# One repeated load taken out, and the startup and the first turn of a fused attention and gated feed-forward kernel put in another order

## The chip, the cores and the metric

The kernel runs on one core of a Trainium2 chip. The metric is the device time of one execution, in microseconds (us). The kernel before takes 296.58 us (median of four runs, 295.89 to 297.06). Times of a stage are read from one profiled execution of each kernel, whose clock starts with the span; a span is about 2 us shorter than the device time.

A core has engines that run side by side: TensorE multiplies matrices, VectorE and ScalarE work on elements, and GpSimd issues most of the loads here. A DMA is a transfer between memories. The granted clock is the share of TensorE's full speed that the profile shows, 1.00 or 0.50 here. A warming product is a matrix product whose result is not used.

Runs of one and the same kernel differ here by up to 2%. Over four jobs the kernel before gave 292.4 to 298.1 us. A good part of what follows is about the reason, so single microseconds are compared only between kernels that ran in one job, or stage by stage in the profiles. All runs compared are "fast", which here means within 1.5% of the fastest run of the same kernel.

## The reference

```python
# attention: window of 16 around each position, plus 24 block summaries (max of k, mean of v)
scores_l = scale * q @ k.T;  masked where |i-j| >= 16
scores_s = scale * q @ k_sum.T + log(32)
a = softmax(concat(scores_l, scores_s));  attn = a @ concat(v, v_sum)
# gated feed-forward on x = attn, 3072 tokens x 512
out = x + sigmoid(x @ w_res) * ((gelu(x @ w_gate) * (x @ w_val)) @ w_out)
```

There are 4 batches, 8 heads, 768 positions of 64 dimensions, and 1536 inner features.

## The kernel before

The work is cut into 8 units, each half a batch (384 tokens). A unit is: scores and exponentials for four head pairs, attention products, transposes of the normed result `xn` into `xT`, twelve blocks of gate and value products (`g`, `vv`), then residual products (`r`) and output products (`f`). While one unit's `r` and `f` run, the next unit's attention is woven in; I call this the turn. In these traces TensorE takes its matmuls in the order of the program (in the changed kernel a transpose whose input is ready at 20.25 starts at 22.16, behind a product that waits), so an order of statements is an order of waits.

Unit 0 has nothing to be woven into. Its attention is the startup. This is its second half, as it was before:

```python
        firsts = [(w, fo, None) for fo in range(2) for w in (w_gate, w_val)]
        for hp in range(NP):                       # four head pairs
            av_part(0, hp, st, blocks=True)        # TensorE: attention products with the block summaries
            av_norm(hp, st)                        # VectorE: reciprocal and multiplication -> xn
            if hp:
                xt_step(0, hp - 1, st, *(AO if hp % 2 else TT), nc.scalar.copy)   # TensorE transposes, ScalarE copies
            if hp > 1:
                firsts = [(w, fo, half_fo(st, w, fo, hp - 2, hp - 1, acc)) for w, fo, acc in firsts]
        firsts = [(w, fo, half_fo(st, w, fo, NP - 2, NP - 1, acc)) for w, fo, acc in firsts]
        xt_step(0, NP - 1, st, *TT, nc.scalar.copy)
        # ... constants ...
        load_batch(1)
        load_batch(1)
```

The transpose of pair `hp - 1` stands behind the block products of pair `hp`, and the gate and value products of pair `hp - 2` stand behind that transpose. So while ScalarE copies one transposed pair, TensorE has another pair's work.

`load_batch(1)` stands twice. Each call takes the next buffers of its pool, and the program reads what the second call loaded. In the startup's first half two of the four pairs' scores are masked by VectorE after the exponential, and two by adding a large negative mask in the accumulator with a TensorE product (`ident` times `nmask`).

The softmax here doesn't subtract the row's maximum and nothing guards it: scores larger than these inputs give would overflow.

## Time and profile before

| stage (from the timeline) | from | to | us |
|---|---|---|---|
| startup: first transpose of k to `g` of the third inner block | 6.99 | 28.66 | 21.67 |
| unit 0's other inner blocks, to the first scores of the turn | 28.66 | 42.87 | 14.21 |
| unit 0's turn, to unit 1's first `g` | 42.87 | 59.83 | 16.96 |
| unit 1, to unit 2's first `g` | 59.83 | 102.29 | 42.46 |

The windows view of the kernel before for these four stages. Columns: the stretch, its length, busy time of each engine with its number of instructions, then the granted TensorE clock, the share of the DMA engines and GB/s.

```profile
6.99:28.66 21.67, 17.03 (x280) 9.87 (x280) 12.65 (x50) 12.33 (x21) 15.68 (x22) 0.76 1.80 182
28.66:42.87 14.21, 14.21 (x112) 8.43 (x112) 8.92 (x18) 6.16 (x14) 6.64 (x8) 1.00 1.32 203
42.87:59.83 16.96, 14.07 (x158) 7.31 (x158) 9.38 (x21) 8.39 (x11) 6.97 (x9) 1.00 1.97 179
59.83:102.29 42.46, 38.34 (x386) 20.51 (x388) 23.91 (x59) 20.43 (x30) 13.87 (x18) 0.92 1.61 166
```

Of these four stages, the clock is under 1.00 in the startup and in unit 1. On the page of the kernel before, the rows of busy tenths of TensorE and of its clock say where, in 40 slices of 7.4 us:

```profile
PE   8589996949999999999999999999999999999993
...
PEclk9867999987999999999999999999999999999998
```

From the tenth slice to the last but one TensorE is busy for 90% or more of each.

The chain of waits of the kernel before, in unit 1 (start, length, what):

```profile
54.68 10.43 DMA k_sb<-in_k_dram
...
65.15 0.85 PE tp L174 x16
66.00 1.39 PE g L295 x4
```

TensorE had nothing left to do at about 61.3 and stood until the second copy of batch 1's k had landed at 65.15. The four gate products after the transposes take 1.39 us, about twice the 0.65 of a dense unit: the clock is at half. In the GpSimd timeline of the kernel before both loads can be seen, the first one long before it is needed and never read, the second behind the seven value loads of the first call:

```profile
31.17 0.79 POOL L87 DMA_DIRECT2D k_sb<-in_k_dram  x1 [0.46 <-DMA w_val<-in_moe_w_val_dram]
...
54.68 0.79 POOL L87 DMA_DIRECT2D k_sb<-in_k_dram  x1 [4.05 <-PE xp L282]
```

The chain of waits of the kernel before in the second half of the startup:

```profile
21.29 0.57 DVE xn L273
...
21.90 0.34 PE xp L282 x3
22.25 0.32 PE ao L263 x12
...
22.98 0.32 PE g L295
...
27.03 0.18 PE xp L282 x3
...
27.23 0.49 ACT xT L284
...
28.66 0.48 PE g L295 x2
```

Between 21.90 and 27.03 nearly every piece is TensorE's own work. Only the last copy (0.49) is waited for. The windows view for the two clock windows around it shows what the clock did:

```profile
19.35:22.77 3.42, 2.47 (x47) 1.41 (x46) 1.89 (x6) 1.44 (x4) 2.69 (x4) 1.00 1.46 199
22.77:26.18 3.41, 3.41 (x26) 1.76 (x24) 1.49 (x6) 0.96 (x2) 1.91 (x3) 0.50 1.45 194
```

### The profile page before, as it was taken

How to read it: one execution, taken by the hardware profiler on the slowest of the kernel's cores; microseconds unless marked ns; L12 is line 12 of the kernel's file. 1: busy time of each engine (PE TensorE's matmuls, PEld its weight loads, DVE VectorE, ACT ScalarE, POOL GpSimd, SP SyncE). 2: the span in 40 equal slices, each digit the busy share in tenths (PEclk: the TensorE clock that was granted, in tenths of full speed). 3: DMA queues.
4: the chain of work that ended last, by engine and by line, in shares of the span. 5: the costliest groups of instructions: out<-in, count | busy, mean ns of one | idle time of the engine just before them, and what ended most of it. 6: DMA issues, size and time to landing. Idle time of an engine off the chain costs nothing.

```text
span 294.4 us, 6276 instructions
## 1 busy us (share of the span) xinstructions
PE 275.7 (94%) x2602; PEld 149.8 (51%) x2624; DVE 174.6 (59%) x431; ACT 138.4 (47%) x214; POOL 52.3 (18%) x74
## 2 busy tenths in 40 slices
PE   8589996949999999999999999999999999999993
PEld 3444553525555555555554555555554565456541
DVE  3745734635556787387655786386655784575333
ACT  2853459004646443564656433654655434643410
POOL 7965632543620300013000000000000000000000
PEclk9867999987999999999999999999999999999998
DMA  6999999999999380009000110001000110010001
GB/s 91 168 184 196 201 206 205 148 234 165 195 137 191 88 85 0 2 36 129 2 0 3 71 38 1 2 36 73 2 0 3 71 38 0 2 71 38 0 36 71
DMA packets 51867, 23.72 MB, mean 81 GB/s; under 512 B 32128, under 2 KB 48768, under 8 KB 51840
## 3 DMA queue, kind: packets, MB, share of 16 engines
q0 software_dynamic: 48384, 17.04, 58.4%
q1 hardware_dynamic: 3456, 6.29, 5.7%
q8 instruction: 20, 0.33, 0.5%
q14 instruction: 7, 0.06, 0.1%
HBM read 34.08 MB, written 6.29 MB: 137 GB/s over the span
## 4 chain that ended last, share of the span: by engine, by line
PE 89%; DMA 4%; ACT 3%; DVE 2%; issue 1%; DVEq 0%; ACTq 0%
PE g L295 23%; PE vv L295 21%; PE f L323 19%; PE r L313 7%; PE tp L174 4%; PE ao L263 4%; DMA k_sb<-in_k_dram 4%; PE s L239 3%; PE vs L204 3%; PE xp L282 2%; PE wp L337 2%; ACT P L243 1%; PE s L232 1%; ACT kW L181 1%; ACT L243 0%
## 5 line engine op out<-in xcount | busy, mean ns | idle before, releaser
L295 PE MATMUL g<-xT,w_gate 128*128 128x384 bf16 x384 | 82.6, 332 | 0.7 <-ACT xT L284 0.6
L301 ACT ACTIVATE ge<-g 128x384 f32<-128x384 f32 x96 | 47.0, 491 | 73.5 <-DVE gvT L302 38.8
L302 DVE TENSOR_TENSOR gvT<-ge,vv 128x384 bf16<-128x384 f32 x96 | 53.0, 553 | 46.3 <-PE vv L295 44.4
L295 PE MATMUL vv<-xT,w_val 128*128 128x384 bf16 x384 | 80.5, 330 | 0.0
L323 PE MATMUL f<-w_out,gvT 128*128 128x512 bf16 x274 | 65.7, 379 | 1.4 <-issue 1.0
L295 PEld LDWEIGHTS <-w_val 128*128 128x128 bf16 x384 | 38.0, 99 | 26.9 <-issue 2.9
L295 PEld LDWEIGHTS <-w_gate 128*128 128x128 bf16 x384 | 35.4, 99 | 24.6 <-issue 3.5
L323 PEld LDWEIGHTS <-gvT 128*128 128x128 bf16 x288 | 27.1, 98 | 30.4
L243 ACT ACTIVATE P<-s,bias_t 128x768 bf16<-128x768 f32 x32 | 28.9, 902 | 28.7 <-PE s L239 28.6
L96 POOL DMA_DIRECT2D vext<-in_v_dram x35 | 28.8, 827 | 60.7 <-PE ao L263 41.9
L247 DVE TENSOR_TENSOR P<-P,maskt 128x768 bf16<-128x768 bf16 x30 | 16.7, 556 | 18.4 <-ACT P L243 18.4
L313 PE MATMUL r<-w_res,xT 128*128 128x512 bf16 x88 | 24.4, 381 | 0.4
L328 DVE SCALAR_TENSOR_TENSOR th<-th,f 128x512 f32<-128x512 f32 x24 | 16.3, 681 | 8.9 <-PE f L323 8.9
L181 ACT COPY kW<-tp 128x768 bf16<-128x768 bf16 x16 | 12.8, 801 | 18.0 <-PE tp L174 18.0
L273 DVE TENSOR_TENSOR xn<-ao,rz 128x384 bf16<-128x384 f32 x32 | 17.8, 558 | 1.1
L316 ACT ACTIVATE th<-r 128x512 f32<-128x512 f32 x24 | 14.3, 595 | 8.8 <-PE r L313 8.4
L195 ACT COPY qT<-tp 128x768 bf16<-128x768 bf16 (+1 forms) x20 | 13.3, 676 | 8.4 <-PE tp L174 8.4
L263 PEld LDWEIGHTS <-P 128*64 128x64 bf16 (+2 forms) x432 | 10.2, 116 | 13.6 <-DVE P L247 5.1
L330 DVE SCALAR_TENSOR_TENSOR o<-th,xn 128x512 f32<-128x512 f32 x24 | 16.6, 692 | 0.8
L239 PE MATMUL s<-qT,kW 64*128 64x64 bf16 x384 | 11.5, 194 | 3.7 <-DVE kW L191 1.9
L271 DVE RECIPROCAL rz<-ao 128x6 f32<-128x6 f32 x32 | 6.2, 192 | 14.7 <-PE ao L263 14.6
L185 DVE TENSOR_TENSOR km<-kW 128x384 bf16<-128x384 bf16 x16 | 5.7, 353 | 13.5 <-ACT kW L181 13.3
(62 smaller groups left out, 200.9 us busy)
## 6 DMA issues: line engine op xcount, KB each, us to landing
out_dram<-o SPq DMA_DIRECT2D x24, 256.0 KB, 2.1
vext<-in_v_dram POOLq DMA_DIRECT2D x25, 128.0 KB, 12.5
k_sb<-in_k_dram POOLq DMA_DIRECT2D x4, 768.0 KB, 10.0
q_sb<-in_q_dram POOLq DMA_DIRECT2D x4, 768.0 KB, 13.9
w_gate<-in_moe_w_gate_dram POOLq DMA_DIRECT2D x6, 256.0 KB, 8.7
w_val<-in_moe_w_val_dram POOLq DMA_DIRECT2D x6, 256.0 KB, 8.9
w_out<-in_moe_w_out_dram POOLq DMA_DIRECT2D x3, 512.0 KB, 14.1
k_sb<-in_k_dram POOLq DMA_DIRECT2D x2, 384.0 KB, 5.9
```

What stands on the lines that cost most here:

```text
L96: nc.gpsimd.dma_start(out=dst, in_=v[b, :, lo:hi, :].rearrange("h p d -> p h d"))
L239: nc.tensor.matmul(s[:, hh, t * QT:(t + 1) * QT], kw[ps, tt, :], qt[ps, tt * QT:(tt + 1) * QT], start=not first, stop=True, skip_group_che ...
L243: nc.scalar.activation(P.rearrange("p a t q -> p a (t q)"), s[:, :, 0:TU], AF.Exp, scale=scale, bias=bias_t[:])
L247: nc.vector.tensor_mul(Pf, Pf, maskt.unsqueeze(1).to_broadcast([128, 2 * HT, QT]))
L263: nc.tensor.matmul(ao[64 * e:64 * e + 64, sub, hh, :], P[rows, hh, t, :], rhs, start=blocks is None or (not blocks and sub == 0 and hh == ...
L273: nc.vector.tensor_mul(xn, ao[:, :, :, 0:D], rz.to_broadcast([128, NSUB, 2, D]))
L295: nc.tensor.matmul(acc[:, 0:TU], w[:, ko, fs], st["xT"][:, ko, :], start=(ko == 0), stop=(ko == KO - 1))
L301: nc.scalar.activation(ge[:], g[:, 0:TU], AF.Gelu)
L302: nc.vector.tensor_mul(gvT[:, fo, :], ge[:], vv[:, 0:TU])
L313: nc.tensor.matmul(r[:], st["xT"][:, ko, ss], w_res[:, ko, :], start=(ko == 0), stop=(ko == KO - 1))
L323: nc.tensor.matmul(st["f", sub][:], gvT[:, fo, ss], w_out[:, fo, :], start=(fo == 0), stop=(fo == FO - 1))
L330: nc.vector.scalar_tensor_tensor(o[:], th[:], 0.5, st["xn"][:, sub, :], ALU.mult, ALU.add)
```

## The change

It has four parts.

- **Load**: the second `load_batch(1)` goes.
- **Front**: all four first scores are masked by TensorE; 13 warming products at the start and 3 more in the gap ahead of the first scores, in place of 16 at the start; the block means of the values are spread differently.
- **Loop**: block products and norms of all four pairs first, then transpose, copy and products pair by pair.
- **Turn**: in unit 0's turn two residual products come ahead of the second scores, and output products are cut in twos.

```diff
-        keep_warm(16)
+        keep_warm(13)
 ...
-        for hp in range(NP):
+        for hp in range(2):
             k_step(0, hp, *MM)
             q_step(qa, 0, 0, TU, hp, *MM)
-            if hp:
-                s_step(0, hp - 1, st, hp > 2)
-            ...
+        s = mask_step()
+        keep_warm(3)
+        s_step(0, 0, st, s)
+        ...                              # the like for pairs 1 to 3: k and q of the next pair, mask, scores
+        vs = vsum_sum(0, *MM, range(0, 2))
 ...
         for hp in range(NP):
             av_part(0, hp, st, blocks=True)
             av_norm(hp, st)
-            if hp:
-                xt_step(0, hp - 1, st, *(AO if hp % 2 else TT), nc.scalar.copy)
-            if hp > 1:
-                firsts = [(w, fo, half_fo(st, w, fo, hp - 2, hp - 1, acc)) for w, fo, acc in firsts]
-        firsts = [(w, fo, half_fo(st, w, fo, NP - 2, NP - 1, acc)) for w, fo, acc in firsts]
-        xt_step(0, NP - 1, st, *TT, nc.scalar.copy)
+        for hp in range(NP):
+            xt_step(0, hp, st, *(TT if hp % 2 else AO), nc.scalar.copy)
+            if hp < NP - 1:
+                firsts = [(w, fo, half_fo(st, w, fo, hp, hp + 1, acc)) for w, fo, acc in firsts]
 ...
         load_batch(1)
-        load_batch(1)
 ...
                 s_step(n, 0, nst)
                 res_step(st, 0)
+                res_step(st, 1)
                 s_step(n, 1, nst)
-                res_step(st, 1)
+                res_step(st, 2)
                 s_step(n, 2, nst)
+                ffn_step(st, gvT, 0, 0, 2)
                 av_step(n, 0, nst)
-                res_step(st, 2)
+                ffn_step(st, gvT, 0, 2, 4)
 ...
```

More of the change, by code (lines that the diff above doesn't have):

```diff
@@ L224, in vsum_bc, with mask_step, s_step @@
             nc.vector.tensor_copy(vext[b % 2][96:128, lo:hi, 2 * hp:2 * hp + 2, 0:D], src)
-        def s_step(u, hp, st, first=False):
+        def mask_step():
+            s = ps_s.tile([128, 2, 512], F32, tag="s", name="s")
+            for hh in range(2):
+                nc.tensor.matmul(s[:, hh, 0:TU].rearrange("p (t q) -> p t q", t=HT), ident[:],
+                                 nmask.unsqueeze(1).to_broadcast([128, HT, QT]),
+                                 start=True, stop=False, skip_group_check=True)
+            return s
+        def s_step(u, hp, st, s=None):
             b, half = u // 2, u % 2
-            s = ps_s.tile([128, 2, 512], F32, tag="s", name="s")
+            first = s is not None
+            if not first:
+                s = ps_s.tile([128, 2, 512], F32, tag="s", name="s")
             kw, qt = kW[b % 2][hp], qT[b % 2][hp]
-            if first:
-                for hh in range(2):
-                    nc.tensor.matmul(s[:, hh, 0:TU].rearrange("p (t q) -> p t q", t=HT), ident[:],
-                                     nmask.unsqueeze(1).to_broadcast([128, HT, QT]),
-                                     start=True, stop=False, skip_group_check=True)
             for t in range(HT):
@@ L363 @@
         st = new_unit()
-        keep_warm(16)
+        keep_warm(13)
         nc.scalar.activation(pre[:], bias_t[0:1, :], AF.Exp)
-        for hp in range(NP):
+        for hp in range(2):
             k_step(0, hp, *MM)
             q_step(qa, 0, 0, TU, hp, *MM)
-            if hp:
-                s_step(0, hp - 1, st, hp > 2)
-            if hp == 2:
-                v_spread(0, 0, HT // 2, 0)
-        vs = vsum_sum(0, *MM, range(0, 3))
-        s_step(0, NP - 1, st, True)
+        s = mask_step()
+        keep_warm(3)
+        s_step(0, 0, st, s)
+        k_step(0, 2, *MM)
+        q_step(qa, 0, 0, TU, 2, *MM)
+        s = mask_step()
+        s_step(0, 1, st, s)
+        v_spread(0, 0, HT // 2, 0)
+        k_step(0, 3, *MM)
+        q_step(qa, 0, 0, TU, 3, *MM)
+        s = mask_step()
+        s_step(0, 2, st, s)
         v_spread(0, 0, HT // 2, 1)
-        vsum_sum(0, *MM, range(3, 4), vs)
+        vs = vsum_sum(0, *MM, range(0, 2))
+        s = mask_step()
+        s_step(0, 3, st, s)
+        vsum_sum(0, *MM, range(2, 4), vs)
         nc.scalar.activation(pre[:], bias_t[0:1, :], AF.Gelu)
@@ L379 @@
         av_part(0, 1, st, *TT, blocks=False)
+        vsum_sum(0, *MM, range(4, NC + 1), vs)
         two = ps_s.tile([128, 2, 512], F32, tag="s", name="ao2")
@@ L383 @@
             av_part(0, hp, st, blocks=False, home=home)
-        vsum_sum(0, *MM, range(4, NC + 1), vs)
         vsum_out(0, vs, 0, 2, nc.vector.tensor_copy)
@@ L431 @@
                 res_step(st, 0)
+                res_step(st, 1)
                 s_step(n, 1, nst)
-                res_step(st, 1)
+                res_step(st, 2)
                 s_step(n, 2, nst)
+                ffn_step(st, gvT, 0, 0, 2)
                 av_step(n, 0, nst)
-                res_step(st, 2)
+                ffn_step(st, gvT, 0, 2, 4)
                 s_step(n, 3, nst)
+                ffn_step(st, gvT, 1, 0, 2)
                 av_step(n, 1, nst)
-                ffn_step(st, gvT, 0, 0, 4)
                 xt_step(n, 0, nst, *TT)
+                ffn_step(st, gvT, 1, 2, 4)
                 av_step(n, 2, nst)
-                ffn_step(st, gvT, 1, 0, 4)
+                ffn_step(st, gvT, 2, 0, 2)
                 xt_step(n, 1, nst, *TT)
                 av_step(n, 3, nst)
-                ffn_step(st, gvT, 2, 0, 4)
+                ffn_step(st, gvT, 2, 2, 4)
                 xt_step(n, 2, nst, *TT)
```

## The prediction

> **What bounds it now.** TensorE: 94% busy (busy table), 89% of the chain of waits. Units 3 and 5 run dense: 34.29 and 34.28 us from their first gate product to the next unit's (timeline), 34.0 of them busy at clock 1.00 (windows). Three places are not dense, and the change touches each.
>
> 1. Unit 1 takes 42.46 us (59.83 to 102.29). Unit 3 plus the seven block-mean products that unit 1 has in addition (7 x 0.216) is 35.8: 6.65 us are lost. The chain shows the DMA of k_sb until 65.15: TensorE idles 3.9 us, because its transposes read batch 1's second copy of k, issued only at 54.68. Then it runs at clock 0.50 until 70.55. The Trainium skill, "TensorE: Matmul & The Clock Gate", Part 1, says the clock falls to half after an idle window of about 3.4 us; the trace agrees (0.50 for 6.83 us; 128x384 products 0.32 us apart instead of 0.16).
>
> 2. Startup, 6.99 (first transpose) to 27.76 (last step of the first gate products): clock 0.50 from 12.5 to 19.4 and from 22.8 to 26.2 (windows).
>
> 3. Unit 0's turn into unit 1, 42.87 to 59.83: 16.96 us for about 13.6 of TensorE issue (spacing of its products), so 3.3 idle, behind ScalarE's table load (1.28), exponentials (0.90) and tanh (0.60).
>
> **What the change does.**
>
> - The repeated load goes. Batch 1's k then comes from the load issued at 31.17; at the trace's queue rate it lands near 50, before it is wanted (about 58). Wait and throttled stretch both go, all on the critical path: -6.5 us (6.0 to 6.7). This is the sure part.
>
> - Startup. Two mask multiplications leave VectorE (0.56 each); four 128x384 products come to TensorE (0.16 each, 0.40 when throttled); three warming products move into the gap at 8.4 to 10.3, to keep the clock up. ScalarE paces 7 to 15 us (copies 0.80 and 0.48, exponentials 0.90), so little is won there. With the clock up, the fourth exponential starts about 1.2 us earlier and the block products end sooner. But each transpose of xn now stands directly ahead of the products that need its copy: a round costs about 0.9 (transpose to first product, 21.90 to 22.81) plus 4 x 0.16, four rounds some 5.4 to 6 us, the copy exposed each time; before, another head's work covered it. I expect -1.2 us net, between -3.5 and +1.5.
>
> - Unit 0's turn: two residual products cover the table load, but scores still wait for exponentials and attention products for VectorE's norms. I count 3.0 us idle instead of 3.3, with small gains elsewhere: -0.4 us.
>
> Weights arrive about 1.34 us per 256 KB and would limit the startup only if it gained over 4.7 us (residual weights land near 38, wanted at 43.15 before).
>
> **Predicted:** 296.86 - 8.1 = 288.8 us, range 286.0 to 291.2. Faster by over 2%: 0.87; within 2%: 0.13; slower: 0.00.
>
> **What would show it.** Right: no DMA of k in the chain after startup; clock 1.00 in unit 1, which takes 35.6 to 36.2 us; 28 value loads instead of 35. Startup: clock above 0.50 between 12 and 20 us; the last step of the first gate products between 24 and 29 us. Unit 0's turn: 16 to 17 us. Wrong: k_sb still waited for, or values or q newly waited for in unit 1; a longer startup, with xT copies named as releasers.
>
> **What would make it wrong.** The clock's windows start at their own time, so the startup may throttle differently: it may gain 4 us if the clock stays up throughout, or lose if TensorE is at half clock in the transposes' rounds. Earlier TensorE work might run into weights not yet landed.

## The result

The changed kernel takes 292.53 us (median of four runs, 291.99 to 293.62), the one before 296.58. The ratio is 0.987, with a 95% interval of 0.983 to 0.991. It is the mean time of the fast runs of one kernel over that of the other in the same rounds, so not quite the ratio of the medians. That is 4 us gained where 8.1 were forecast, outside the stated range.

The same four stages in the windows view of the changed kernel:

```profile
6.91:31.43 24.52, 18.02 (x286) 10.27 (x287) 11.66 (x48) 12.41 (x21) 17.43 (x26) 0.78 1.80 183
31.43:46.91 15.48, 15.48 (x113) 8.88 (x112) 8.94 (x18) 6.25 (x14) 6.49 (x8) 0.91 1.28 206
46.91:63.68 16.77, 14.15 (x158) 7.09 (x158) 9.17 (x21) 8.28 (x11) 7.34 (x10) 1.00 2.00 180
63.68:99.52 35.84, 35.58 (x384) 19.29 (x386) 23.46 (x58) 20.34 (x30) 4.04 (x6) 1.00 0.80 107
```

| stage | before | changed | difference |
|---|---|---|---|
| startup | 21.67 | 24.52 | +2.85 |
| unit 0's other inner blocks | 14.21 | 15.48 | +1.27 |
| unit 0's turn | 16.96 | 16.77 | -0.19 |
| unit 1 | 42.46 | 35.91 (to unit 2's first `g` at 99.59) | -6.55 |

The sum is -2.62, and the spans differ by 294.4 - 291.9 = 2.5. So nothing large is left to look for elsewhere: unit 1 gained what was forecast, and the startup and the dense stretch behind it gave 4.1 us back.

The page of the changed kernel:

```profile
PE   8867998799999999999999999999999999999993
...
PEclk9995699999999999999999999999999999999998
```

The dip of the clock in unit 1 (slices 9 and 10 of before) is gone. The startup's dip has moved from the second to fourth slice into the fourth and fifth, where the dense products begin.

The chain of waits of the changed kernel in unit 1 no longer has a DMA:

```profile
63.84 0.65 PE g L300 x4
64.49 0.65 PE vv L300 x4
65.14 0.46 PE tp L174 x16
```

The chain of waits of the changed kernel in the second half of the startup:

```profile
21.08 0.57 DVE xn L278
...
21.69 0.54 PE ao L268 x12
22.23 0.45 PE xp L287 x3
...
22.70 0.49 ACT xT L289
...
23.22 0.48 PE g L300
...
25.02 0.49 ACT xT L289
...
27.35 0.49 ACT xT L289
...
29.67 0.49 ACT xT L289
```

Two things are new. The block products of the fourth pair (`ao`, 21.69) wait for the norm of the third pair (`xn`), and the first transpose (`xp`), whose own input was ready at 20.25, stands behind them. Then the copy `xT` is on the chain four times and not once. A round from transpose to transpose takes 2.3 us.

The windows view of the changed kernel, by the windows of the clock, from 17.11 on:

```profile
17.11:20.53 3.42, 2.87 (x88) 1.81 (x88) 1.30 (x5) 2.38 (x4) 3.12 (x5) 1.00 1.45 197
20.53:23.94 3.41, 1.69 (x18) 1.12 (x18) 2.25 (x7) 0.48 (x1) 2.07 (x3) 0.50 1.44 197
23.94:27.35 3.41, 2.80 (x13) 1.47 (x12) 1.16 (x15) 0.48 (x2) 1.69 (x3) 0.50 1.46 197
27.35:30.77 3.42, 2.33 (x9) 1.16 (x9) 0.00 (x0) 1.01 (x3) 2.08 (x3) 0.50 1.45 196
30.77:34.18 3.41, 3.41 (x12) 1.62 (x11) 2.23 (x4) 1.42 (x3) 1.56 (x2) 0.50 1.42 199
```

In this profile the clock stays at half through four windows, 13.65 us, and comes back after the first window in which TensorE has no gap (3.41 of 3.41). The windows with gaps (1.69, 2.80 and 2.33 us busy) did not bring it back. That is not a rule. The windows view of e12_after, the same program run again, has a half-clock window in the same rounds with about as many gaps, and the clock came back after it:

```profile
23.02:26.43 3.41, 2.78 (x11) 1.42 (x11) 1.64 (x17) 0.49 (x2) 2.18 (x3) 0.50 1.45 194
26.43:29.85 3.42, 2.23 (x16) 1.23 (x15) 0.00 (x0) 1.46 (x4) 1.61 (x4) 1.00 1.45 196
```

So what brings the clock back stays open. The Trainium skill, "TensorE: Matmul & The Clock Gate", section "Part 1: The HAM clock gate (the "warmup" mystery)", says that the clock is decided in windows of 3413 ns and that it is either half or full. The trace agrees with both: every change is a multiple of 3.41 us from the last, and only 0.50 and 1.00 occur.

### The profile page after: what moved, and what is told of

It reads as the page before. It is cut to its first block, busy times and chain, and to the rows that moved or that the text cites. A ratio compares the mean times of both kernels' runs of the same rounds, so it can differ in the third digit from the quotient of the medians.

```text
span 291.9 us, 6270 instructions
## 1 busy us (share of the span) xinstructions
PE 275.4 (94%) x2605; PEld 149.1 (51%) x2628; DVE 173.1 (59%) x429; ACT 138.3 (47%) x214; POOL 44.6 (15%) x65
## 4 chain that ended last, share of the span: by engine, by line
PE 88%; ACT 3%; DVE 3%; DMA 2%; POOL 2%; issue 1%; POOLq 0%; DVEq 0%
PE g L300 24%; PE vv L300 22%; PE f L328 21%; PE r L318 7%; PE tp L174 4%; PE ao L268 4%; PE s L244 3%; PE xp L287 2%; PE vs L204 2%; DMA vext<-in_v_dram 2%; DVE xn L278 1%; ACT P L248 1%; ACT xT L289 1%; POOL vext L96 1%; POOL k_sb L87 1%
## 5 line engine op out<-in xcount | busy, mean ns | idle before, releaser
L96 POOL DMA_DIRECT2D vext<-in_v_dram x28 | 23.0, 827 | 61.9 <-PE ao L268 46.9
L252 DVE TENSOR_TENSOR P<-P,maskt 128x768 bf16<-128x768 bf16 x28 | 15.6, 556 | 18.4 <-ACT P L248 18.4
L268 PEld LDWEIGHTS <-P 128*64 128x64 bf16 (+2 forms) x432 | 9.6, 111 | 15.3 <-issue 5.5
L268 PE MATMUL ao<-vext,P 128*64 128x65 bf16 (+1 forms) x384 | 11.8, 199 | 0.9 <-DVE xn L278 0.9
```

What stands on the lines that cost most here:

```text
L96: nc.gpsimd.dma_start(out=dst, in_=v[b, :, lo:hi, :].rearrange("h p d -> p h d"))
L268: nc.tensor.matmul(ao[64 * e:64 * e + 64, sub, hh, :], P[rows, hh, t, :], rhs, start=blocks is None or (not blocks and sub == 0 and hh == ...
```

## The experiments

My theory after the comparison was that the load is worth what was forecast, and that the new loop costs about 4 us, by its exposed copies and by the gaps that keep the clock down (the last point did not hold up as a rule, see above). Rivals were that the load is worth less, that the front only moved the throttled stretch into dense products, and that the light block products throttle the clock, not the gaps.

| run | what | median us | ratio to before | first transpose to third block's `g` |
|---|---|---|---|---|
| e1_R | load | 289.83 | 0.9855 | 21.76 |
| e2_RM | load, front | 287.65 | 0.9782 | 20.57 |
| e3_RB | load, loop | 294.63 | 1.0044 | 24.87 |
| e4_RT | load, turn | 288.56 | 0.9826 | 21.02 |
| e5_RMT | all but the loop | 288.19 | 0.9712 | 21.43 |
| e6_ahead | changed, transposes one ahead | 288.86 | 0.9738 | 21.39 |
| e7_warm | changed, warming products in the waits | 292.04 | 0.9841 | 24.91 |
| e9_norms | changed, norms behind all block products | 289.12 | 0.9803 | 21.61 |
| e10_both | e6 and e9 | 287.13 | 0.9722 | 21.44 |
| e11_held | e10 and five warming products | 287.66 | 0.9731 | 19.64 |
| e12_after | changed, again | 292.64 | 0.9903 | 23.42 |

Runs e1 to e4 were one job (before: 294.18, the median of its six fast runs; 294.98 with the slow one), e5 to e8 the next (before: 296.42), e9 to e12 the third (before: 295.68). The 95% intervals of the ratios are 0.004 to 0.010 to each side, so ratios that differ by less than about 0.007 (two half-widths of 0.005 together) are not told apart by time. All gave correct results.

### The parts one by one

e1_R is before without the repeated load:

```diff
         load_batch(1)
-        load_batch(1)
```

> Before, with the repeated load of batch 1 taken out and nothing else. Theory (the load was worth its whole 6.5 us, and the startup of the changed kernel gives about 4 us of it back): 290.0 us, 6.0 to 6.7 below before; clock 1.00 all through unit 1; the startup as in before, g of the third output block starting near 28.7 us. Rival (the load was worth only the 4 us that the whole change brought): 292.5 us.

It took 289.83 against 294.18, a difference of 4.35 us; the interval of the ratio allows 2.4 to 6.2. So time alone does not tell the 6.0 to 6.7 that I forecast from the rival's 4. The profile says more: unit 1 behaved as foreseen, from 60.20 to 96.11, 35.91 us at clock 1.00. The shortfall may lie on the side of the kernel before, which loses a varying amount there (see e8).

e2_RM has the load and the front, e3_RB the load and the loop, e4_RT the load and the turn; their diffs are those parts of the diff above and nothing else.

> Load out, and the front of the startup as in the changed kernel (masks on TensorE, warming products moved, block means of values moved), but the loop over the four head pairs as before: block products of each pair in its own turn. Theory (the loss comes from the new loop, in which each transposed copy stands exposed): faster than load-out-alone by 0.5 to 2 us, third output block's g starting at 26.5 to 28.5 us. Rival (the loss comes from the front: it only moves the throttled stretch later, into dense products): slower than load-out-alone by 2 us or more, third block's g near 31 us.

> Load out, startup's front as before, and only the new loop: all block products first, then transpose, copy and products pair by pair. Theory (the new loop costs): slower than load-out-alone by 2 to 4 us, four rounds of 1.5 us at full clock or 2.3 us at half, PE gate products waiting for xT copies four times. Rival (the front costs): within 1 us of load-out-alone.

> Load out, startup as before, and only unit 0's turn in the new order (two residual products ahead of the second scores, output products cut in twos). Both theories: 0.1 to 0.5 us faster than load-out-alone; first gate product of unit 1 about 16.7 us after the first scores of the turn, instead of 16.96.

Against e1_R on the same chip, the front gained 2.2 us (287.65), the loop lost 4.8 (294.63), and the turn gained 1.3 (288.56), which time does not tell from nothing. The front's gain and the loop's loss are both a little over what I expected (0.5 to 2 and 2 to 4). The loop is the part that costs: load and loop together are no better than before. The rival that the front is to blame is out. The loop also lowers the clock: the mean granted clocks of the four runs are 0.954 to 0.977 in e3_RB and 0.978 to 0.987 in e1_R. The waits view of e3_RB shows the two new waits of the changed kernel with the old front:

```profile
PE ao L263 <- DVE xn L273: 2.4, 2, 1.6
PE g L295 <- ACT xT L284: 2.3, 4, 0.6
```

Columns are who waited for whom, the us in total, the times and the longest. Four waits for the copy, as said, and one of 1.6 us for a norm.

Of the turn's 1.3 us only 0.2 belong to the turn, which took 16.76 us instead of 16.96 in the profiles. Another 0.7 lies in the startup, which is the same program in e1 and e4 and took 21.76 and 21.02 us, its half-clock windows starting at other times. That is how much luck can do here.

e5_RMT is the changed kernel with the old loop:

> The changed kernel with only its loop over head pairs put back to the old order (load out, front, and unit 0's turn stay new). Theory (the loop is the only part that costs): load-out-alone less 2.2 for the front less 0.2 for the turn, so 286.5 to 288 us, faster than before by over 2%. Rival (the parts interact, the front's gain needs the new loop): no faster than 289.5 us.

It took 288.19, just above the 286.5 to 288 expected and under the rival's 289.5. The ratio is 0.971: over 2% faster than before, and faster than the changed kernel (0.987). The front's gain does not need the new loop.

### What in the loop costs

e6_ahead keeps all block products first, and moves only the transposes:

```diff
-        for hp in range(NP):
-            xt_step(0, hp, st, *(TT if hp % 2 else AO), nc.scalar.copy)
-            if hp < NP - 1:
-                firsts = [...]
+        xt_step(0, 0, st, *AO, nc.scalar.copy)
+        for hp in range(NP - 1):
+            xt_step(0, hp + 1, st, *(AO if hp % 2 else TT), nc.scalar.copy)
+            firsts = [...]
```

> The changed kernel, block products of all pairs still first, but each transpose of xn issued one pair ahead, so that one pair's products cover the next pair's copy. Theory (the loop costs because its copies stand exposed, and the gaps keep the clock down): most of the loss comes back, 288 to 290 us; two to three windows at half clock instead of four, no or one wait of gate products for xT. Rival (block products first is itself what costs, by a stretch of light matmuls that throttles the clock): 291.5 us or more.

It took 288.86 (0.974), so nearly the whole loss is recovered, with block products still first. Block products first are not by themselves the cause. The chain of waits of e6_ahead has one copy instead of four, and then TensorE without a gap, at 0.32 us a product until 27.3 and 0.16 after:

```profile
22.50 0.49 ACT xT L289
...
23.03 0.48 PE g L300
...
26.07 0.32 PE xp L287 x3
26.39 0.32 PE g L300
...
27.57 0.18 PE g L300
```

Half clock lasted two windows (20.51 to 27.33) and not four.

e7_warm leaves the copies exposed and fills the waits:

```diff
+        wr = ps_s.tile([128, 2, 512], F32, tag="s", name="wr")
         for hp in range(NP):
             xt_step(0, hp, st, *(TT if hp % 2 else AO), nc.scalar.copy)
+            for i in range(2):
+                nc.tensor.matmul(wr[:, 0, :], warm[:, 0:128], warm[:], start=True, stop=True)
```

> The changed kernel with two warming products of 128x512 (results unused) after each of the four transposes, in the wait for the copy: the copies stay exposed, only the clock sees a busy TensorE. If the clock is part of the cost: full clock back by about 27.4 us instead of 34.2 and the kernel 1.5 to 3 us faster than the changed one, 289.5 to 291 us. If the exposed copies alone cost: no change or up to 0.5 us slower, 292.5 to 293 us.

It took 292.04 (0.984 against 0.987 and 0.990 for the changed kernel), which is not told apart from it by time. The profile says more. The clock did come back after two windows, at 28.82, and the third block's `g` was as late as before (24.91 us after the first transpose, 24.52 in the changed kernel), but the dense blocks behind it ran at full clock: the turn began 39.03 us after the first transpose of k instead of 40.00. So what the clock costs in the dense stretch is about 1 us in these two profiles; the rest is in the rounds, where half clock and waits act together. Whether the warming products brought the clock back is not shown: e12_after, without them, was at half for one window in its rounds and began its turn 37.70 us after the first transpose of k. My 1.5 to 3 us were too much; the first round grew by the warming product itself, which had to wait for the last norm.

e9_norms takes away the other new wait, with the data and the arithmetic unchanged:

```diff
         for hp in range(NP):
             av_part(0, hp, st, blocks=True)
+        for hp in range(NP):
             av_norm(hp, st)
```

> The changed kernel with one edit: the four norms are issued after all four block products, not in turn with them. In the changed kernel the fourth block products wait 1.5 us for the third pair's norm (both pairs share one tile of accumulators), and the first transpose stands behind them. If that wait is part of the loss: first transpose at about 20.3 us instead of 22.2, rounds as before, kernel 1 to 2 us faster than the changed one. If the exposed copies alone set the pace: no change.

> The changed kernel once more, on the same chip as the other three, as the yardstick: 292 to 293.5 us, third output block's g near 31 us, 10 to 14 us at half clock.

On one chip e9_norms took 289.12 and the changed kernel 292.64 (290.87 to 294.19), ratios 0.980 and 0.990; one of the four runs of e9_norms (291.47) lies among those of the other. The first transpose came at 20.34 instead of 22.17. Those 1.8 us are all that the two profiles differ by (spans 287.5 and 289.2, startups 21.61 and 23.42). The medians differ by 3.5; two of the four runs of e12_after, which were not profiled, had mean clocks of 0.971 and 0.973 and took 294 us, so the rest goes with the clock. The expectation for e12_after missed in the profile: 6.8 us at half clock, in two windows apart, and not 10 to 14, and the third block's `g` at 29.89 and not near 31. Pairs 2 and 3 have their accumulators in one tile, and I take it that a product for pair 3 issued after a read for pair 2 is therefore made to wait for it. That the shared tile is the reason was not tested apart; that the order makes the wait was.

The chain of waits of e9_norms also gives the price of a round at either clock:

```profile
20.41 0.29 PE xp L287 x3
...
22.65 0.34 PE xp L287 x3
...
24.93 0.18 PE xp L287 x3
...
26.47 0.18 PE xp L287 x3
```

A round takes about 2.3 us at half clock (2.24 and 2.28, the first of them in part at full) and 1.54 at full.

e10_both has both edits:

> That edit and the transposes one pair ahead together. Theory: the two losses add, so 1 to 2 us faster than transposes-ahead alone: 287 to 288 us, third output block's g at 26.3 to 27.3 us. Rival (products at half clock set the pace once copies are covered): 288.5 to 289 us.

It took 287.13 (0.972), 2 us better than e9_norms but not clearly better than e6_ahead (0.974, another job). Its profiled run was at half clock from 16.06 to 26.30, and had its first transpose at 22.23 after all. The third block's `g` came at 28.01 and not at 26.3 to 27.3. Whether the two losses add is not settled. The median is what the theory said, but two runs took 285.8 and 286.0 us and two 288.3 and 288.9; the profiled one is of the second kind and looks as the rival said: TensorE without gaps at half clock, its own products the pace.

e11_held puts three warming products ahead of the last block means and two ahead of the block products:

```diff
+        keep_warm(3)
         vsum_sum(0, *MM, range(4, NC + 1), vs)
 ...
         vsum_out(0, vs, 2, 8, nc.scalar.copy)
+        keep_warm(2)
```

> As the last one, with five warming products more (three ahead of the last block means, two ahead of the block products), in the stretch of light matmuls of 17 to 20.5 us after which the clock falls. If these light matmuls are what throttles: no half clock between 20.5 and 27.3 us, third output block's g near 24.5 to 25.5 us, 285 to 286.5 us. If the window falls otherwise: 0 to 0.5 us slower than the last one.

In the profiled run the clock was at 1.00 until 285.10 of 285.3 us, and the startup took 19.64 us, the least of the runs in the table. The third block's `g` came at 26.13, later than the 24.5 to 25.5 expected. By time it is not better than e10_both (287.66 and 287.13). Its four runs had mean clocks of 1.000, 0.987, 0.997 and 0.991, so in two of them the clock fell all the same: five products are not enough in every run. The warming products also stand in TensorE's order and hold up what follows.

### Why the kernel before spreads

e8_before is one look at the kernel before, once more; its state is unknown. (The text says on another chip: it ran on the chip of e1 to e7; which chip the first profile came from is not recorded.)

> The kernel before once more, unchanged, for its profile on another chip: its times here spread from 292.4 to 298 us. All theories: the wait for batch 1's k in unit 1 and the half clock after it again; if the spread comes from that wait, its length differs from 3.9 us by over 0.5 us; if from the clock's windows in the startup, the third output block's g differs from 28.7 us by as much.

The windows view of e8_before for its unit 1 (a stretch that reaches 1.5 us into unit 2) and for two clock windows:

```profile
59.66:101.80 42.14, 38.77 (x393) 20.74 (x395) 25.02 (x62) 20.83 (x31) 13.71 (x17) 0.96 1.91 175
65.18:68.59 3.41, 3.41 (x26) 1.70 (x24) 1.83 (x6) 1.68 (x3) 0.00 (x0) 0.50 1.53 217
44.70:48.11 3.41, 3.41 (x30) 1.36 (x31) 0.91 (x3) 2.32 (x4) 0.87 (x1) 0.50 1.24 207
```

Unit 1 ended with the next `g` at 100.31, after 40.65 us and not 42.46: TensorE's wait for k was 3.1 us, and only one window of unit 1 was at half clock instead of two. So the load is worth 6.55 us in one execution and 4.7 in the other, by the same account (less 35.91). The startup was shorter too (19.36 us instead of 21.67, though it began 0.7 later), and a window of the turn, 44.70 to 48.11, ran at half clock, which it does not in the other profile (turn 18.38 us instead of 16.96). The same program thus moves by one to two microseconds in each of three places, and a difference of that size between the startups of two profiles proves nothing; the repeated runs of e1 to e4 do the work there.

## Why the prediction was wrong

The prediction named the right places and the right signs for two of three, and failed in the size and the sign of the startup.

- **The load: right.** Forecast -6.5 us, with clock 1.00 and unit 1 in 35.6 to 36.2 us. Unit 1 took 35.91, at 1.00, with no DMA in the chain and 28 value loads, against the 42.46 of the very profile that was forecast from. By time the load alone gave 4.35 us (e1_R, interval 2.4 to 6.2). The wait and its half-clock windows are not the same in every run of the kernel before: e8_before gives 4.7. The "6.0 to 6.7" was read from one profile and was too narrow.
- **The startup: wrong, and the whole miss.** "I expect -1.2 us net, between -3.5 and +1.5": it was +2.85, and +1.27 more in the dense stretch behind it, +4.1 in the profile. The experiments split it into -2.2 for the front and +4.8 for the loop, +2.6 together by time. The remaining 1.5 us to the profile's 4.1 are within what two executions of one program differ by.
- **Where this step failed.** The mechanism stood in the text ("the copy exposed each time; before, another head's work covered it"), and its price at full clock was right: 0.9 plus 4 x 0.16 is 1.54, and e9_norms shows 1.54. But the sum of four rounds was taken at full clock, "some 5.4 to 6 us". In the profile of the changed kernel they ran at half, at 2.3 us each, from 22.16 until the third block at 31.43: 9.3 us, where the old loop took 6.8 (21.90 to 28.66). In e12_after, the same program, two rounds ran mostly at half and two at full: 7.7 us (22.17 to 29.89). Of the 4.1 us lost, 2.5 are these rounds, 1.3 the dense stretch at half clock behind them, and 0.3 a later first transpose. So the failed term is the cost of the four rounds, priced at a clock that they did not have. This is not chance alone, since the loop lowers the clock: e3_RB against e1_R shows it, and the eight runs of the changed kernel had 0.971 to 0.988 where e5_RMT, with the old loop, had 0.986 to 1.000. These eight runs are also ordered by it: 290.87 and 291.36 us at 0.988, 292.0 to 292.6 at 0.982, 293.6 to 294.2 at 0.971 to 0.974. At about equal clock the loop still costs some 2 us (289.18 at 0.986 in e5_RMT, 290.87 and 291.36 at 0.988; an estimate, as they are of different jobs and chips); the rest of the 4.4 us between the medians goes with the clock. Why the loop lowers the clock is not shown. My idea was that the exposed copies are gaps, and that gaps keep the clock from coming back. But it did come back after windows with 2.78 (e12_after) and 2.84 us busy (e9_norms), and stayed down after one with 3.37 (e5_RMT, 20.26 to 23.67).
- **A wait that was not seen.** The fourth block products waited 1.53 us for the third norm and held up the first transpose (e9_norms: 20.34 instead of 22.17). It could have been read from the program: a norm of pair 2 stands ahead of a write to the tile that it shares with pair 3.
- **The front: better than its part in the sum.** In the profile of the changed kernel the clock did stay up until 20.53, as intended, and the fourth exponential started at 16.63 instead of 17.44. That is 0.8 us, where 1.2 was forecast. In part that was luck: of nine profiles with the new front, three (e2_RM, e10_both, e12_after) fell to half before 20 us, but so did all five with the old one. The front gained 2.2 us by time (e2_RM against e1_R).
- **The turn: right in sign, small.** Forecast -0.4, measured -0.19 (16.96 to 16.77), and 0.2 in e4_RT.
- **What would show it wrong** did show it: "a longer startup, with xT copies named as releasers". "Lose if TensorE is at half clock in the transposes' rounds" stood among the risks. It should have been the middle of the forecast, because TensorE had been at half clock in these very rounds before.

A version better than both came out of it: the changed kernel with the old loop (e5_RMT, 0.971), and equally the new loop with transposes one ahead and norms behind the block products (e10_both, 0.972). They are not told apart. What stays open is why a given window throttles, what brings the clock back, and so which of these two would win over many runs.

## What to carry to other kernels

When statements on an in-order engine are regrouped by kind (all of this, then all of that), ask of each what now stands between it and the copy that it needs; a transpose should be issued one step ahead of the products that read its copy. Price a stage at both clocks when its clock is not known, and compare the granted clocks of several runs, because one profile shows one draw: the same program spent 13.65 us of its startup at half clock in one profile and 6.8 in another. Take apart a change with several parts before trusting its sum: here a gain of 4 us hid a loss of nearly 5.

## What the Trainium skill lacked or had wrong

- "TensorE: Matmul & The Clock Gate", Part 1, gives "after ≥1 idle window (~3.4µs)" for the fall of the clock. Here it fell after a window in which TensorE was busy for 2.87 of 3.42 us (17.11 to 20.53, changed kernel), with small matmuls (96 or 32 rows by 64 columns for the attention), after one with 2.47 busy (before, 19.35 to 22.77), and in unit 1 of before after one with 0.98. The page's section "HAM oscillation — how this bites in real kernels" speaks of idle gaps over about 3.4 us; in the first of these windows only 0.55 us were idle in all. The page also names short idles between groups of products, but without an amount. The busy share alone does not decide: windows with 2.31 and 2.32 us busy (changed kernel, 10.29 to 17.11) were followed by full clock. What counts as activity is not said. Five more products of 128x512 in that stretch went with a clock that stayed up in one profiled run (e11_held), which would fit a weight by the size of a product, but this was not tested by itself.
- The same page's "After ≥1 busy SHORT window" for its return does not say how busy. Windows with 1.69, 2.80 and 2.33 us busy (changed kernel) and 3.37 (e5_RMT) did not bring it back; windows with 2.78 (e12_after), 2.84 (e9_norms) and 3.41 did.
- The page says that for modelling the ramp is under 1% of a typical kernel's span. It says so of the first ramp; here the clock fell again inside the kernel, and the eight runs of the changed kernel took 290.87 to 294.19 us with mean clocks of 0.988 down to 0.971, a spread of 1.1% that goes with the clock.
